# Attention and two mixtures on one core: transposes behind the first scores, the last root ahead of four scatters, and another last block

## The chip, the core and the metric

The kernel runs on one core of a Trainium2 chip. The core has a tensor engine (PE, with its weight loads shown apart as PEld), a vector engine (DVE), a scalar engine (ACT), GpSimd (POOL) and a queue engine (SP), each with its own instruction queue, worked through in order. Engines wait for one another by semaphores. The metric is the device time of one execution in microseconds (us).

## What is computed

```python
scores = np.where(mask, -1e9, scale * np.matmul(q, k.transpose(0, 1, 3, 2)))   # 4 x 12 heads, 448 x 448, 64 wide
attn = softmax(scores); x = np.matmul(attn, v)        # joined to x: 1792 rows of 768
# first mixture: 8 experts, w1 [8, 768, 1024], w2 [8, 1024, 768]
xn = x / (np.linalg.norm(x, axis=-1, keepdims=True) + 1e-06)
en = expert_emb / (np.linalg.norm(expert_emb, axis=-1, keepdims=True) + 1e-06)
logits = xn @ en.T / tau
# each row goes to the expert of its largest logit, gate_w is its probability
out[mask] = gate_w[mask, None] * (np.maximum(x[mask] @ w1[e], 0.0) @ w2[e])
# second mixture on that output: logits = x @ w_gate + modality_bias[modality_id], the same form
```

## The kernel before

All products are made of float32 numbers split into a high and a low part, so that one product is three matmuls (high by high, low by high, high by low). The order of the instructions is the order in which the program is written, on each engine.

**Attention.** A loop over `g` takes the 24 pairs of heads as a pipeline: in one round, `qk(g, c)` makes the scores of pair g in four chunks of 112 rows (L401 and, for the mask, L403 on PE), `rowmax` (L408, DVE) and `expo` (L413, ACT) follow them, `last_chunk` (transposes L435 on PE, `ph` L438 on ACT, `pl` L440 on DVE) and `values` (L468) work on earlier pairs, and `route_t` on a still earlier one. The scores stand in a pool of PSUM banks, and the transposes take two other banks in turn, one of which the embeddings' transposes (`enT_ps`) also use.

**Routing beside it.** What the first mixture needs for its choice of experts is written as generators, of which a round takes single steps with `tick()`. A `yield ALIGN` sets `hold`: the next step is only taken at `tick(True)`, which stands right behind the first two `qk` chunks of a round. `prep_en` normalizes the eight expert embeddings and transposes them on PE (L343); `route_root(b)` makes the reciprocal norms of batch b's rows from their sums of squares: for the last batch an add on DVE (L549), then `root2`, which starts with a power on POOL (L153, `rt_sr`) and goes on with small DVE instructions (L157, L159, L161, L163), and two more (L551, L553) that leave `r1nr`. The routing of a batch ends in scatters of its rows' places to a table in memory (L622 clears a column, L623 is the scatter on POOL).

**The mixtures.** Blocks of 128 rows that share an expert follow one another. A block's rows are gathered, transposed (L909), split into `xh` (ACT, L911) and `xl` (DVE, L912), multiplied with the first weights (L927, L928, L929, eight groups of 128 columns), and `down` multiplies with the second weights (`o`, L989), takes the gate in with two activations of 384 columns (L994, ACT) and scatters 128 rows of 768 to the output (L999, POOL). The first block of the first mixture opens while the routing of the last batch is being done; its `xl` stands on DVE behind `drain(route_root(B - 1))`, the root of the last batch.

**The end.** Sections run over up to 21 blocks, the last seven in nested tests of the number of blocks (L1306). With this data 17 blocks run. Behind the sections a flag `cl` tells whether the last block needs new second weights; the program tests it on all engines but PE (L1314) and splits them if so, and `down` for the last block follows on both ways.

Of the kernel before, what the change touches and what calls it, by code (L numbers as in the profile page):

```python
# [23 lines left out]
P = 128  # L24
# [31 lines left out]
def attention_two_moe_kernel(  # L56
# [225 lines left out]
    def drain(gen):  # L282
        for _ in gen:
            pass
# [42 lines left out]
    def prep_en():  # L327
        jk = xb_p.tile([CP, D], F32, tag="jk", name="ebj", bufs=2)[:E]
        ss = small.tile([E, 1], F32, tag="ess", name="ess")
        act.activation(jk, eb, AF.Square, accum_out=ss)  # L330
        yield
        nr = small.tile([E, 1], F32, tag="enr", name="enr")
        yield from root2(nr, ss, E, 1, "en")
        vec.tensor_scalar(out=nr, in0=nr, scalar1=0.5, scalar2=1e-6, op0=ALU.mult, op1=ALU.add)
        yield
        vec.reciprocal(nr, nr)
        yield
        vec.tensor_scalar_mul(jk, eb, nr)
        yield
        yield  # L340
        pt = ps_t.tile([P, KD, E], F32, tag="t", name="enT_ps")
        for c in range(KD):
            pe.transpose(pt[:, c], jk[:, c * P : (c + 1) * P], ident[:E, :E])  # L343
        yield
        for k in range(2):
            vec.tensor_copy(enT[:, :, k, :E], pt)
        vec.tensor_sub(enT[:, :, 0, E:], pt, enT[:, :, 0, :E].bitcast(F32))
        vec.tensor_copy(enT[:, :, 1, E:], zero8[:, None, :].to_broadcast([P, KD, E]))
# [179 lines left out]
    def route_ss(b, c, xb, part=0):  # L528

        cut = D - 2 * HD  # L530
        lo, hi = ((0, D), (0, cut), (cut, D))[part]
        if b not in sss:
            sss[b] = small.tile([CP, 2, NCH], F32, tag="r1ss", name=f"r1ss{b}")
        jk = xb_p.tile([CP, D], F32, tag="jk", name=f"r1jk{b}{c}{part}", bufs=2)
        acc = sss[b][:, part // 2, c : c + 1]
        if part == 2:
            vec.tensor_tensor_reduce(out=jk[:, lo:hi], in0=xb[:, c, lo:hi], in1=xb[:, c, lo:hi], scale=1.0, scalar=0.0,
                                     op0=ALU.mult, op1=ALU.add, accum_out=acc)
        else:
            act.activation(jk[:, lo:hi], xb[:, c, lo:hi], AF.Square, accum_out=acc)  # L540
# [140 lines left out]
    def split_w(which, his=None, los=None):  # L681
        drain(split_steps(which, his, los))
# [80 lines left out]
    for g in range(NPR + 3):  # L763
        t, v, r = g - 1, g - 2, g - 3
        if r == 0:
            drain(routing)
            routing = None
            vec.tensor_scalar_mul(tau_h, tau_t, 0.5)
            for b in range(B):
                vec.tensor_copy(mts[b][:, :, 3], mod_i[:, b * NCH : (b + 1) * NCH, 0])  # L770
        if 0 <= v < NPR and v % PB == 0:
            xbs[v // PB] = xb_p.tile([CP, NCH, D], F32, tag="xb", name=f"xb{v // PB}")
        late = [last_chunk(t, e) if 0 <= t < NPR else iter(()) for e in range(2)]
        if g < NPR:
            for c in range(2):
                qk(g, c)
        tick(True)
        if g < NPR:
            for c in range(2):
                both(rowmax, g, c)  # L780
            for c in range(2):
                both(expo, g, c, ticks=False)
        if g == NPR + 1:
            split_w(1, (), (2, 3))
        if g == NPR + 2:
            split_w(1, (), (4, 5))
        if 0 <= t < NPR:
            halves_lo(t)
        next(late[0], None)
        if NPR <= g:  # L790
            warm(ps_T, "T", WT)
        if 0 <= r < NPR:
            if r == NPR - 1:
                for c in range(NCH):
                    route_ss(B - 1, c, xbs[B - 1], 2)
            route_t(r, xbs[r // PB])
            if r == NPR - 2:
                for c in range(NCH):
                    route_ss(B - 1, c, xbs[B - 1], 1)
        next(late[0], None)  # L800
        if 0 <= v < NPR:
            if g > NPR - 1:
                warm(ps_T, "T", WV)
            values(v, 0)
        next(late[0], None)
        if PB <= r < NPR and r % PB < NCH:
            b = r // PB - 1
            c = -1
            for c in ((0,), (1,), (2,), (3,))[r % PB] if b < B - 2 else ((0,), (1,), (2, 3), ())[r % PB]:
                store_x(b, c)  # L810
                route_ss(b, c, xbs[b])
            if c == NCH - 1:
                drain(routing or ())
                routing = route1(b)
        if g < NPR:
            for c in range(2, NCH):
                qk(g, c)
                both(rowmax, g, c)
            for c in range(2, NCH):
                both(expo, g, c, ticks=False)  # L820
        next(late[1], None)
        if 0 <= v < NPR:
            values(v, 1)
        next(late[1], None)
        next(late[1], None)
        if 0 <= r < NPR:
            route_l(r)
        if 0 <= v < NPR:
            combine(v, xbs[v // PB])
        if g < NPR:  # L830
            halves_hi(g)
        if g + 4 < NPR:
            load_pair(g + 4)
        if g + 3 < NPR:
            load_v(g + 3)
        if g + 2 < NPR:
            split_pair(g + 2)
        if g + 1 < NPR:
            split_v(g + 1)
        if LEAD <= g <= NPR:  # L840
            for c in range(g - LEAD, KD if g == NPR else g - LEAD + 1):
                load_lead(m1, 1, c)
        if g == NPR - 1:
            st_q.close()
            ps_h = left("ps_h", 2, space=PSUM)
            ps_T = left("ps_T", 2, space=PSUM)
        if g == NPR:
            st_x.close()
            wb = left("wb", 1)
            w1h = [wb.tile([P, F], F32R, name=f"w1h{c}") for c in range(KD)]  # L850
            w1l = [wb.tile([P, F], F32R, name=f"w1l{c}") for c in range(KD)]
            w2r = [wb.tile([P, D], F32, name=f"w2r{f}") for f in range(KF)]
            m1.gather_early((0,), 2 * S)
            load_lead(m1, 2)
        if g == NPR:
            for k in range(2):
                pcopy(w1h[k], w1r[k])
            split_w(1, (2, 3, 4, 5), (0, 1))
# [24 lines left out]
    lgs2 = [wq.tile([P, 1, E], F32, name=f"lg{i}") for i in range(2)]  # L883
    mxs = [wq.tile([P, 1], F32, name=f"mx{i}") for i in range(2)]
    gt = wq.tile([P, MW], F32, name="gt")
    mes = [wq.tile([P, MW], F32, name=f"me{i}") for i in range(2)]
    KH = KF // 2
    hl, hh = ([wq.tile([P, KH, P], F32R, name=f"h{t}{i}") for i in range(2)] for t in "lh")
# [94 lines left out]
    def down(m, mg, then=None, between={}):  # L983
        ops = ps_a.tile([P, 2, 512], F32, tag="av", name="o")
        for f in range(KF):
            between.get(f, lambda: None)()
            for w, h, st in ((w2h, hh, 0), (w2l, hh, 1), (w2h, hl, 2)):
                for n in range(2):
                    pe.matmul(ops[:, n, :384], lhsT=h[f // KH][:, f % KH], rhs=w[f][:, n * 384 : (n + 1) * 384],  # L989
                              start=(f == 0 and st == 0), stop=(f == KF - 1 and st == 2))  # L990
        if then:
            then()
        for n in range(2):
            act.activation(yb[:, n * 384 : (n + 1) * 384], ops[:, n, :384], AF.Copy, scale=mg[:, 2:3])  # L994
        if m.routed:
            if then:
                pass_on()
            vec.tensor_copy(ym, mg)
        pool.indirect_dma_start(out=x1 if m.routed else out, out_offset=IND(ap=mg[:, 1:2].bitcast(I32), axis=0),  # L999
                                in_=yb, in_offset=None, bounds_check=NT - 1, oob_is_err=False)  # L1000

    def route_t2():
        for k in range(2):
# [229 lines left out]
    def run(m, is_full):  # L1233
# [72 lines left out]
        with ExitStack() as ifs:  # L1306
            for j in range(1, MAXB):
                if j == NBLK - 1:
                    total = nc.values_load(tab[0:1, 3, 0:1], min_val=NBLK, max_val=MAXB)
                    cl = nc.values_load(tab[0:1, 1, 0:1], engines=WE, min_val=0, max_val=1)  # L1310
                if j >= NBLK:
                    ifs.enter_context(tc.If(total > j))
                section(j)
        with tc.If(cl > 0):  # L1314
            split_w(2)
            if follow:
                load_lead(follow, 2)
        if follow:
            route_t2()
            follow.gather_early((0,), what="x")  # L1320
            split_w(1, range(3), ())
            drain(route_a())
            pass_on()
        if not follow:
            return down(m, gt)

        def middle():
            route_l2()
# [37 lines left out]
        yield  # L1366
        table(m1, None)

    drain(route_root(B - 1))
    m1.gather_early((1,), 3 * S)  # L1370
    open_phase(m1, m1.is_full(), last_route1, 2)
    is_full = run(m1, None)
# [41 lines left out]
```

## Time and profile before

| | |
|---|---|
| three runs | 974.64, 973.98, 970.02 us, median 973.98 |
| the profiled execution | 971.22 us, of it 969.5 from the first to the last instruction (the span) |
| mean granted clock of PE | 0.973 |
| busy in the span | PE 876.3, DVE 696.4, POOL 475.3, ACT 430.5 us |

Times in the profile are microseconds from the start of the span. A row of a timeline gives the start, the busy time, the engine with line and operation, output and inputs, and in brackets the idle time of the engine ahead of it with the instruction that ended it. A name with a q behind it (ACTq) is an engine's queue, where jumps, loads of registers and semaphores are.

### The profile page before, as it was taken

To read this page: it belongs to the slowest core of one execution; us is meant where nothing else is said; L and a number is where in the kernel's file an instruction comes from. 1 tells how busy PE (TensorE), PEld (TensorE's weight loads), DVE (VectorE), ACT (ScalarE), POOL (GpSimd) and SP (SyncE) were. 2 spreads that over 40 slices of the span, in tenths; PEclk is the share of its full clock that TensorE was granted. 3 is DMA by queue.
4 is the path that set the end of the run, shared out by engine and by line. 5 is a ranking of instruction groups with operands and counts; after the bars stand their busy time and mean duration, and the time that the engine had idled before them with its cause. 6 is when DMAs were issued, how large, how long until landed. Compare 5 with 4: busy or idle time off the path is not lost. (4 is left out here: it accounts for less than half of the span.)

```text
span 969.5 us, 20969 instructions
## 1 busy us (share of the span) xinstructions
PE 876.3 (90%) x7034; PEld 760.5 (78%) x7034; DVE 696.4 (72%) x1789; ACT 430.5 (44%) x777; POOL 475.3 (49%) x476
## 2 busy tenths in 40 slices
PE   5788898989868899999999999998989999899994
PEld 3677776767547788898989988886879998789894
DVE  6788888888764768689746965348767579996660
ACT  3565766857433565466525643234111234422111
POOL 8576655883135634464543564422545453463530
PEclk9999999999979899999999999999989999999997
DMA  6568796978915775468614662111172114411110
GB/s 186 121 134 164 159 188 130 197 179 167 262 47 183 283 291 177 172 222 307 223 45 165 221 205 83 46 33 38 53 266 82 50 52 165 152 51 38 63 40 31
DMA packets 112870, 137.45 MB, mean 142 GB/s; under 512 B 76800, under 2 KB 81200, under 8 KB 112704
## 3 DMA queue, kind: packets, MB, share of 16 engines
q1 hardware_dynamic: 99840, 108.75, 40.0%
q0 software_dynamic: 12864, 26.83, 8.7%
q8 instruction: 62, 1.02, 0.4%
q14 instruction: 104, 0.85, 0.3%
HBM read 101.48 MB, written 19.92 MB: 125 GB/s over the span
## 5 line engine op out<-in xcount | busy, mean ns | idle before, releaser
L728 POOL DMA_INDIRECT xg<-x,xi x128 | 134.1, 1047 | 99.0 <-DMA x<-yb,mg 50.1
L927 PE MATMUL h<-w1h,xh 128*128 128x512 f32 x408 | 165.9, 407 | 2.7 <-issue 1.9
L929 PE MATMUL h<-w1h,xl 128*128 128x512 f32 x408 | 162.2, 398 | 6.3 <-DVE xl L912 6.0
L928 PE MATMUL h<-w1l,xh 128*128 128x512 f32 x408 | 162.3, 398 | 3.0 <-DVEq L1226 2.6
L989 PE MATMUL o<-w2h,hh 128*128 128x384 f32 x544 | 145.4, 348 | 5.4 <-ACTq L1314 3.9
L989 PE MATMUL o<-w2l,hh 128*128 128x384 f32 x544 | 142.9, 344 | 4.9 <-issue 2.6
L989 PE MATMUL o<-w2h,hl 128*128 128x384 f32 x544 | 142.5, 343 | 2.3 <-issue 1.2
L969 DVE STREAM_TRANSPOSE hs<-h 32x256 f32<-32x256 f32 x240 | 107.0, 446 | 24.7 <-PE h L929 13.4
L413 ACT ACTIVATE ex<-sc,nm 112x112 f32<-112x112 f32 (+1 forms) x192 | 83.8, 492 | 76.5 <-DVE nm L408 75.3
L989 PEld LDWEIGHTS o<-w2l,hh 128*128 128x128 f32 x544 | 100.3, 192 | 6.9 <-issue 3.9
L989 PEld LDWEIGHTS o<-w2h,hh 128*128 128x128 f32 x544 | 98.9, 193 | 8.0 <-ACTq L1314 4.2
L989 PEld LDWEIGHTS o<-w2h,hl 128*128 128x128 f32 x544 | 100.7, 192 | 3.6 <-issue 1.8
L929 PEld LDWEIGHTS h<-w1h,xl 128*128 128x128 f32 x408 | 77.6, 190 | 25.3 <-DVE xl L912 6.8
L975 ACT ACTIVATE hh<-hs 128x512 fp32r<-128x512 f32 x30 | 18.5, 630 | 175.7 <-PE o L989 135.9
L928 PEld LDWEIGHTS h<-w1l,xh 128*128 128x128 f32 x408 | 77.8, 191 | 19.9 <-DVEq L1226 3.3
L927 PEld LDWEIGHTS h<-w1h,xh 128*128 128x128 f32 x408 | 77.9, 191 | 19.0 <-issue 3.7
L678 DVE TENSOR_TENSOR w1l<-w1r,w1h 128x1024 fp32r<-128x1024 f32 x66 | 76.6, 1220 | 11.3 <-issue 7.9
L408 DVE TENSOR_REDUCE nm<-sc 112x1 f32<-112x112 f32 (+1 forms) x192 | 75.6, 439 | 10.1 <-PE sc L403 9.5
L678 DVE TENSOR_TENSOR w2l<-w2r,w2h 128x768 fp32r<-128x768 f32 x82 | 72.5, 951 | 5.1 <-ACT w2h L676 3.8
L900 DVE STREAM_TRANSPOSE xr<-xg 128x768 f32<-128x768 f32 x32 | 52.1, 1628 | 30.9 <-DMA xg<-x,xi 18.7
L676 ACT CAST w1h<-w1r 128x1024 fp32r<-128x1024 f32 x64 | 62.5, 1046 | 11.1 <-DMA w1r<-in_w1a 3.7
L999 POOL DMA_INDIRECT out<-yb,mg x13 | 16.5, 1272 | 95.2 <-ACT yb L994 95.2
(296 smaller groups left out, 1936.3 us busy)
## 6 DMA issues: line engine op xcount, KB each, us to landing
w1r<-in_w1a SPq DMA_DIRECT2D x48, 512.0 KB
w2r<-in_w2a SPq DMA_DIRECT2D x64, 384.0 KB
r<-in_kqP SPq DMA_DIRECT2D x24, 448.0 KB
w1r<-in_w1b SPq DMA_DIRECT2D x18, 512.0 KB
w2r<-in_w2b SPq DMA_DIRECT2D x24, 384.0 KB
vr<-in_vh SPq DMA_DIRECT2D x24, 224.0 KB
x<-xb SPq DMA_DIRECT2D x16, 336.0 KB
xg<-x,xi POOLq DMA_INDIRECT x128
```

The source lines that it names most:

```text
L408: vec.tensor_reduce(out=nms[h][:, c : c + 1], in_=scs[h, c][:, : CP * (c + 1)], axis=AX.X, op=ALU.min)
L413: act.activation(dst, scs.pop((h, c))[:, :n], AF.Exp, bias=nms[h][:, c : c + 1], scale=-1.0)
L676: act.copy(hi[k], r[k])
L678: vec.tensor_sub(lo[k], r[k], hi[k].bitcast(F32))
L728: pool.indirect_dma_start(out=xgs[j % 3][:, q * (D // Q) : (q + 1) * (D // Q)], out_offset=None, in_=quarters, in_offset=IND(ap=xi[:, q : ...
L900: vec.transpose(xr.rearrange("p k (q r) -> p q k r", q=Q), xgs[j % 3].rearrange("p (q r k) -> p q k r", q=Q, k=KD))
L927: pe.matmul(hps, lhsT=xh[:, c], rhs=w1h[c][:, ns], start=(c == 0), stop=False)
L928: pe.matmul(hps, lhsT=xh[:, c], rhs=w1l[c][:, ns], start=False, stop=False)
L929: pe.matmul(hps, lhsT=xl[:, c], rhs=w1h[c][:, ns], start=False, stop=(c == KD - 1))
L969: vec.transpose(hr[cols, :, rows], hps[rows, q * 256 : (q + 1) * 256].rearrange("p (c k) -> p k c", c=QR))
L975: act.activation(hh[k], part, AF.Relu)
L989: pe.matmul(ops[:, n, :384], lhsT=h[f // KH][:, f % KH], rhs=w[f][:, n * 384 : (n + 1) * 384], start=(f == 0 and st == 0), stop=(f == KF - ...
```

## The change

Three edits. In `prep_en`, the second of two bare `yield`s becomes `yield ALIGN`. In the round where the last pair is routed, `route_root(B - 1)` is made and its first step taken ahead of `route_t`, and the old place drains the rest of it. At the end of the second mixture, `cl` is loaded on PE too, and the last block has its own `down_last`, written out in both ways of a test for `cl < 1`: all matmuls of the first 384 columns, then all of the second, each half with its own activation (the second into the tile `yT`) and its own scatter of 128 rows of 384 to the output seen as 3584 rows, by indices `two` = 2 x row + half.

```diff
@@ prep_en
-        yield
+        yield ALIGN
         pt = ps_t.tile([P, KD, E], F32, tag="t", name="enT_ps")
@@ the loop over g
             if r == NPR - 1:
                 for c in range(NCH):
                     route_ss(B - 1, c, xbs[B - 1], 2)
+                last_root = route_root(B - 1)
+                next(last_root)
             route_t(r, xbs[r // PB])
...
-    drain(route_root(B - 1))
+    drain(last_root)
@@ new
+    two = [wq.tile([P, 1], I32, name=f"two{i}") for i in range(2)]
+    def down_last(m, mg):
+        ops = ps_a.tile([P, 2, 512], F32, tag="av", name="o")
+        yhs = yb[:, :384], yT.rearrange("p k c -> p (k c)")[:, :384]
+        for n in range(2):
+            vec.tensor_scalar(out=two[n], in0=mg[:, 1:2].bitcast(I32), scalar1=2.0, scalar2=float(n), op0=ALU.mult,
+                              op1=ALU.add)
+        for n in range(2):
+            cols = slice(n * 384, (n + 1) * 384)
+            for f in range(KF):
+                for w, h, st in ((w2h, hh, 0), (w2l, hh, 1), (w2h, hl, 2)):
+                    pe.matmul(ops[:, n, :384], lhsT=h[f // KH][:, f % KH], rhs=w[f][:, cols],
+                              start=(f == 0 and st == 0), stop=(f == KF - 1 and st == 2))
+            act.activation(yhs[n], ops[:, n, :384], AF.Copy, scale=mg[:, 2:3])
+            i = pool.indirect_dma_start(out=out.rearrange("n (k d) -> (n k) d", k=2), out_offset=IND(ap=two[n], axis=0),
+                                        in_=yhs[n], in_offset=None, bounds_check=2 * NT - 1, oob_is_err=False)
+            apart(i.ins, "out")
@@ run
-                    cl = nc.values_load(tab[0:1, 1, 0:1], engines=WE, min_val=0, max_val=1)
+                    cl = nc.values_load(tab[0:1, 1, 0:1], engines=WE if follow else WE + [ENG.PE], min_val=0, max_val=1)
...
+        if not follow:
+            with tc.If(cl < 1) as same:
+                down_last(m, gt)
+            with same.Else():
+                split_w(2)
+                down_last(m, gt)
+            return
         with tc.If(cl > 0):
             split_w(2)
-            if follow:
-                load_lead(follow, 2)
+            load_lead(follow, 2)
...
-        if not follow:
-            return down(m, gt)
```

On PE, this is the program at the start of pair 2, before: the transposes of the embeddings (L343) stand between a transpose of pair 1 (L435) and the first scores of pair 2.

```order
L435 MATMUL t<-ident,ex_211 112x112 x4
L343 MATMUL enT_ps<-ident,ebj 128x8 x6
L401 MATMUL sc_0_505<-hi_392 112x112
L401 MATMUL sc_0_506<-hi_392 112x112
L401 MATMUL sc_0_505<-lo_393,hi_392 112x112
```

And with the change, the rows at the other end of those scores: L343 has moved behind all 20 rows of the chunks 0 and 1, ahead of the next transpose L435.

```order
L403 LDWEIGHTS identb
L403 MATMUL sc_1_508<-mask,identb 112x112
L403 LDWEIGHTS identb
L403 MATMUL sc_1_509<-mask,identb 112x112
L343 MATMUL enT_ps<-ident,ebj 128x8 x6
L435 MATMUL t<-ident,ex_212 112x112 x4
```

On POOL, this is the queue ahead of the first mixture, before: two splits of first weights (L143), four clears and scatters of the batch ahead of the last, and the power of the last batch's root (L153) behind them.

```order
L143 TENSOR_SCALAR w1h_5530<-w1r_314 128x1024
L143 TENSOR_SCALAR w1h_5531<-w1r_315 128x1024
L622 MEMSET pad 128x1
L623 DMA meta_63<-mt_115,r1sir_5771 14336x8
L622 MEMSET pad 128x1
L623 DMA meta_63<-mt_115,r1sir_5771 14336x8
L622 MEMSET pad 128x1
L623 DMA meta_63<-mt_115,r1sir_5771 14336x8
L622 MEMSET pad 128x1
L623 DMA meta_63<-mt_115,r1sir_5771 14336x8
L153 TENSOR_TENSOR rt_sr_5891<-r1ss_5623,half 112x4
```

And with the change: the power stands ahead of all eight (on DVE, L549 moves with it, from behind L272 to ahead of L507).

```order
L143 TENSOR_SCALAR w1h_5530<-w1r_314 128x1024
L143 TENSOR_SCALAR w1h_5531<-w1r_315 128x1024
L153 TENSOR_TENSOR rt_sr_5794<-r1ss_5623,half 112x4
L622 MEMSET pad 128x1
L623 DMA meta_63<-mt_115,r1sir_5771 14336x8
```

On ACT, the end of the program with the change: behind the test (L1336, the place of L1314 before) come the two halves of the way without new weights, a jump, and the other way. Before, the eight casts (L676) stood in the test alone, and the two activations (L994) behind it.

```order
L1336 COMPARE_AND_BRANCH
L1018 ACTIVATE yb<-o,gt 128x384
L1018 ACTIVATE yT<-o,gt 128x384
L1336 UNCONDITIONAL_BRANCH
L676 CAST w2h_5887<-w2r_5542 128x768
```

## Rows read from the trace of the kernel before

**Rows 1.** Page, busy us, share of the span, instructions

```profile
PE 876.3 (90%) x7034; PEld 760.5 (78%) x7034; DVE 696.4 (72%) x1789; ACT 430.5 (44%) x777; POOL 475.3 (49%) x476
```

**Rows 2.** Waits of PE in the attention, 0 to 265 (total, times, longest)

```profile
PE t L435 <- DVE xb L487: 10.5, 15, 0.8
```

**Rows 3.** Timeline of PE at the start of pair 2

```profile
29.92 0.81 PE L343 MATMUL enT_ps<-ident,ebj 8*128 8x8 f32 x6 [6.43 <-DVE pl L440]
...
31.76 0.53 PE L401 MATMUL sc<-hi 64*112 64x224 f32 x2
...
32.59 0.44 PE L403 MATMUL sc<-mask,identb 112*112 112x112 bf16 x2
```

**Rows 4.** Timeline of PE in the first block of the first mixture

```profile
272.37 0.77 PE L927 MATMUL h<-w1h,xh 128*128 128x512 f32 x1
272.94 0.63 PE L928 MATMUL h<-w1l,xh 128*128 128x512 f32 x1
279.62 0.80 PE L929 MATMUL h<-w1h,xl 128*128 128x512 f32 x1 [6.05 <-DVE xl L912]
```

**Rows 5.** Timeline of DVE ahead of that block

```profile
268.56 0.62 DVE L507 TENSOR_TENSOR xTl<-t,xTh 128x448 fp32r<-128x448 f32 x1
...
271.62 0.14 DVE L549 TENSOR_TENSOR r1ss<-r1ss 112x4 f32<-112x4 f32 x1
277.18 0.17 DVE L157 TENSOR_SCALAR rt_rr<-rt_sr 112x4 f32<-112x4 f32 x1 [5.41 <-POOL rt_sr L153]
...
277.79 0.16 DVE L163 TENSOR_TENSOR r1nrr<-rt_rr,rt_sr 112x4 f32<-112x4 f32 x1
...
279.00 1.02 DVE L912 TENSOR_TENSOR xl<-xt,xh 128x384 fp32r<-128x384 f32 x2 [0.57 <-DVE r1nrr L553]
```

**Rows 6.** Timeline of PE, start of the last block's second product

```profile
949.53 1.01 PE L989 MATMUL o<-w2h,hh 128*128 128x384 f32 x2 [3.91 <-ACTq L1314]
```

**Rows 7.** Timeline of DVE around pair 2

```profile
23.36 1.70 DVE L163 TENSOR_TENSOR enr<-rt_ren,rt_sen 8x1 f32<-8x1 f32 x1
...
29.24 0.62 DVE L440 SCALAR_TENSOR_TENSOR pl<-t,ph 112x448 f16<-112x448 f32 x1 [1.13 <-ACT ph L438]
...
31.13 0.18 DVE L348 CAST enT<-zero 128x48 fp32r<-128x48 f32 x1
...
32.97 0.69 DVE L408 TENSOR_REDUCE nm<-sc 112x1 f32<-112x224 f32 x2 [0.74 <-PE sc L403]
```

**Rows 8.** Timeline of POOL around pair 2

```profile
22.98 2.07 POOL L146 TENSOR_TENSOR lo<-r,hi 128x896 fp32r<-128x896 f32 x1
```

**Rows 9.** Timeline of ACT around pair 2

```profile
28.14 0.63 ACT L413 ACTIVATE ex<-sc,nm 112x448 f32<-112x448 f32 x1 [0.93 <-DVE nm L408]
```

**Rows 10.** Timeline of POOL ahead of the first mixture

```profile
271.31 1.03 POOL L623 DMA_INDIRECT meta<-mt,r1sir  x1 [20.54 <-DVE ld_rowm L268]
...
276.11 1.04 POOL L153 TENSOR_TENSOR rt_sr<-r1ss,half 112x4 f32<-112x4 f32 x1
```

**Rows 11.** Windows: length, busy of each engine (instructions), PE clock, DMA share, GB/s

```profile
269.39:283.04 13.65, 6.97 (x26) 4.51 (x25) 6.23 (x40) 3.07 (x6) 5.29 (x9) 0.50 0.05 15
949.53:955.48 5.95, 5.95 (x19) 5.79 (x19) 0.00 (x0) 0.00 (x0) 0.00 (x0) 0.50 0.05 19
955.48:960.90 5.42, 5.42 (x31) 5.09 (x30) 0.00 (x0) 0.00 (x0) 0.00 (x0) 1.00 0.00 0
963.80:965.00 1.20, 0.00 (x0) 0.00 (x0) 0.00 (x0) 0.00 (x0) 0.00 (x0) 1.00 0.64 259
```

**Rows 12.** Queue instructions of L1309 (ns min/median/max, first and last start)

```profile
L1309 PEldq TENSOR_LOAD <-t_tabm x1: 308/308/308, 892.3 to 892.3; - x1
```

**Rows 13.** Queue instructions of L1306 from 940 to 952

```profile
L1306 PEldq COMPARE_BRANCH  x2: 186/1820/3453, 942.3 to 946.0; - x2
...
L1306 ACTq EVENT_SEMAPHORE  x2: 17/17/17, 949.0 to 949.1; - x2
L1306 DVEq EVENT_SEMAPHORE  x2: 21/21/21, 949.5 to 949.6; - x2
```

**Rows 14.** Timeline of ACT at the end

```profile
960.99 1.05 ACT L994 ACTIVATE yb<-o,gt 128x384 f32<-128x384 f32 x2 [14.05 <-PE o L989]
```

**Rows 15.** Queue instructions of L1410, end of the program, 960 to 970

```profile
L1410 POOLq DRAIN  x3: 46/113/6547, 962.1 to 969.2; - x3
```

**Rows 16.** Waits of PE from 283 to 345, the longest

```profile
PE h L927 <- issue: 1.9, 2, 1.1
PE pr L1044 <- DVE oh L199: 1.2, 1, 1.2
```

## The prediction

> **What bounds the kernel now.** The page comes first [rows 1]: PE, the tensor engine, is busy for 876 of 969.5 us, so the time can only fall where PE stands idle or runs slowly, and each part of the change is priced at the idle stretch of PE that it touches. The waits of PE in the attention (0 to 265 us) show one of 0.7 us in each of fifteen pairs, on DVE's L487 [rows 2]; they return with the loop, so what PE gains in one pair isn't waited away in the next. The other views are timelines at three places. *Pair 2*: PE stands idle for 6.43 us ahead of the embeddings' transposes, L343 [rows 3]. *Opening of the first mixture*: PE waits 6.05 us ahead of the first L929 [rows 4], for `xl` on DVE (L912), which ends a chain that waited 5.41 us for POOL's power `rt_sr` (L153) [rows 5]. *End*: 3.91 us of idle ahead of the last block's matmuls [rows 6], and a serial tail behind them.
>
> **Part (a), ALIGN in `prep_en`.** Nothing is added or removed. Six transposes (0.81 us) go from ahead of the first two QK chunks of pair 2 to behind them, and three casts on DVE go behind one row maximum. The transposes need the PSUM bank that `pl` (L440) frees at 29.24+0.62 = 29.86 [rows 7]; the QK chunks, which stand behind them, don't. They run from the transposes' end, 29.92+0.81 = 30.73, to 32.59+0.44 = 33.03 [rows 3]. When could they run? Their operands are split by POOL at 22.98+2.07 = 25.05 [rows 8]. Chunk 0 needs two score banks that ACT's exponentials free early, chunk 1 the one that the exponential of 28.14+0.63 = 28.77 frees [rows 9]. So chunk 0 goes into the idle stretch whole, and chunk 1 starts at 28.8 and takes 33.03-31.76 = 1.27 [rows 3]: 30.07. The transposes, by then free of their wait, end at 30.85, where QK ended at 33.03 before: 2.2 us less, of which **I take 2.0** for a start 0.2 later. The casts on DVE ended 31.13+0.18-30.73 = 0.58 behind the transposes [rows 7], so now at 31.4, and hold chunk 1's maximum until about 31.65; before it started at 32.97 [rows 7]. DVE and ACT thus gain 1.3 where PE gains 2.0, and if they pace pair 2, 1.3 is what stays. Bounds: 0 (pairs 3 and 4 wait for loads or splits instead) and 2.2.
>
> **Part (b), the last root ahead of the scatters.** On POOL the power goes past four memsets and the four scatters from 271.31 to just ahead of 276.11, where it took 1.04; POOL had been idle for 20.54 us before them [rows 10]. Its input, the sums of squares, is complete when DVE reaches L507 at 268.56; the add L549, 0.14 us, now comes ahead of that [rows 5]. So the power runs from 268.75 to 269.8, in idle time. DVE's six instructions from L157 on keep their place behind that of L549, where DVE is free at 271.62; they start there and not at 277.18, 5.5 us earlier, take 1.25 us to 278.43 as before (L912 at 279.00 follows the last by 0.57), and `xl` starts at about 273.45 [rows 5]. Its other input, `xh`, is a cast of PE's transposes and is done by 273: PE's first matmul on it ran at 272.37 and the next at 272.94 [rows 4]. PE's L929 goes to about 274.15 from 279.62 [rows 4]: **5.4 us**. Costs: 0.14 for the add ahead of L507, since PE waits for L507's `xTl`; and the power now runs beside DVE's L507. How such a pair fares: L163 on 8 numbers took 1.70 us at 23.36 [rows 7] while POOL's subtraction `lo` ran from 22.98 to 25.05 [rows 8]; the same line took 0.16 at 277.79 with POOL at rest [rows 5]. DVE is held for as long as POOL works, here at most 1.04 us. I take 0.25 of it, since L507 starts with the power or ahead of it and has one input in PSUM: **5.0 us**. The scatters end 1.1 us later, at 277.1; PE waits for none of them by [rows 4, 16], and the next scatters hang on the chain that has moved forward, as all of the last batch's route does.
>
> The Trainium skill ("SBUF — State Buffer", SBUF: two separate sides) states the same as an exclusive lock between a GpSimd operation and a DVE operation with two SBUF inputs, held for the whole instruction; the rows agree (1.70 against 0.16), and by it in full this part would give 5.4-0.14-1.04 = 4.2 in place of 5.0.
>
> The clock adds a bound. PE was granted 0.50 (1.2 GHz) from 269.39 to 283.04 [rows 11], until 3.42 us behind its restart at 279.62. With less idle ahead of it, the return can come earlier behind the restart, or later. The last block prices it: 19 matmuls in 5.95 us at 0.50 and 31 in 5.42 at 1.00 [rows 11], 0.313 against 0.175 each, so a us at the low level does 0.56 us of work, and 3.42 us can give 1.5 back. I take nothing. Bounds of (b): 3.6 (block and add in full, and 0.6 for a later return) and 6.9.
>
> **Part (c), the last block.** One scalar load on PE is added at section 13, 0.31 us by the one beside it [rows 12], under matmuls that are queued there; uncovered it would cost those 0.31. *Start:* PE was ready after its own jump (3.453 us, begun at 942.3 under matmuls) and a branch of 0.19 at 946.0 [rows 13], so at 946.2, and waited for ACT behind L1314 until 949.53 [rows 6]. ACT's events of the sections jumped over come at 949.0 and 949.1, and DVE's, which only the second matmul wants, at 949.5 [rows 13]. Now the test behind L1314 falls through and those events are enough: PE starts near 949.1, **0.4 earlier**. Two new index operations on DVE lie under 11 us of matmuls. *Order:* the 48 matmuls are the same, half after half; the low clock of their first 5.95 us stays, and where it falls can move up to 19 x (0.313-0.175) = 2.6 either way; I take nothing. *Tail:* ACT evicted two halves in 1.05 behind the last matmul [rows 14]; the first now lies under the second half's matmuls, **0.5 less**. The scatter behind it moves half the bytes. Before, packets ran for about 1.2 us at 259 GB/s [rows 11], so this is worth 0.6 if the drain on POOL, from 962.1 for 6.547 us [rows 15], ends with the landing, and 0 if it counts from its start. I take **0.25**. Sum 1.15; bounds 0.5 and 1.5 without the clock.
>
> **Sum.** -2.0 -5.0 -1.15 = -8.15. From the profiled execution's time, 971.22, that gives 963.1; from the median of the three runs, 973.98, it gives 965.8. The profiled execution lies inside those runs (970.02 to 974.64), so I take the middle of the two: **964.4**, from a start of 972.6.
>
> **Rivals.**
> *1. (b) is half given back:* PE gets `xl` early, but some us on it waits for what doesn't hang on the root: splits of the second weights on ACT and DVE, gathers on POOL. For it: those engines do a long list of work there, and their loads were issued on time for the old start. Against: PE's waits from 283 to 345 are 1.2 us and less [rows 16], so no second wait lies close behind the first. -5.65: 966.9.
> *2. (a) carries nothing:* the next pairs are paced by splits on POOL, which fill it there [rows 8]. Against: all that PE waits for later in the attention are the 0.7 us of [rows 2]. -6.15: 966.4.
> *3. The change doesn't do what it says in (b):* the power also reads sums that ACT accumulates, and stands in POOL's queue behind splits of the first weights; if one of them is late, DVE waits on as before. Against: POOL had done with those splits 20.54 us before its scatters [rows 10]. -3.15: 969.4, within 0.5%.
> *4. The other side, PE's clock.* The thin work of 270 to 274 now lies directly ahead of the dense work, and 1.2 GHz may last longer than 3.42 us behind the restart. Each such us loses 0.44. After 18.5 us of longer low clock, to about 296, the 8.15 are gone; past 30 us, to about 307, the kernel is over 0.5% slower, 979 or more. Against it: after the longer idle of before, the high level was back 3.42 us behind the restart [rows 4, 11].
> *5. Better:* the clock returns at once in (b), -1.5 more: 962.9.
>
> The new jumps are a risk inside the range: a jump of 3.453 us on PE, ready at 946.2, would put its start to 949.65 and cost 0.55 [rows 13]. The Trainium skill ("Runtime: NRT & Kernel Launch", Instruction fetch mechanics) states that a taken branch to a target outside the fetched window stalls for the fetch; that row agrees, 3.453 beside a branch of 0.19, and one such stall on PE's new branch would make the sum 7.6 in place of 8.15.
>
> **Chances.** Forecast (963 to 966) 0.50; rival 1 0.18; rival 2 0.12; rival 3 0.09; rival 4 0.03; rival 5 0.08. About 0.5%, 4.9 us, is what a measurement of this kernel can tell from no change: faster is below 969.1. Forecast and rivals 1, 2 and 5 make 0.88, of which 0.04 (the slow edges of 1 and 2) falls to no change: faster 0.84, same 0.13, slower 0.03. The range, 960.5 to 969.0, leaves out rivals 3 and 4 and the far edge of 5.
>
> **What would show it.** (a): L343 stands behind QK chunk 1, no idle of 6.4 us ahead of it, and pair 2 ends some 2 us earlier, as does the attention. (b): POOL's L153 near 269 for about 1.05 us; no wait of 5.4 at L157; the 6.05 ahead of L929 under 1. (c): PE's idle ahead of the last block near 3.5 us, and one eviction behind the last matmul. I'm wrong where such a wait is only renamed: idle of PE of like size within 40 us behind it, or a low clock that lasts much beyond 279.

## The result: 965.6 us, 0.991 of before, and where it came from

The changed kernel took 965.61 us (median of 20 runs, 959.33 to 971.42), the one before, beside it, 973.93 (20 runs, 967.82 to 980.4). The ratio is 0.9913, 95% interval 0.9892 to 0.9933: faster by 8.3 us, more than 0.5%. Forecast were 964.4 us in a range of 960.5 to 969.0. A second measurement on another chip gave 0.9939 (0.9915 to 0.9963), 5.9 us: so the gain is 6 to 8 us, and that the first measurement lies within 0.2 us of the forecast's 8.15 is in part luck.

The profiled execution of the changed kernel has a span of 966.8 us at a mean granted clock of 0.967, against 969.5 at 0.973. These 2.7 us are not the gain, since the two executions differ in their clock where the change has no part. From 40 to 262 us the changed kernel's has 20.5 us at the low level (0.50 granted) and the other 6.8; from 600 to 940 us it has 10.2 against 13.7. At the 0.44 us that the prediction reckons lost in a us at the low level, that is an estimated 4.5 us against the changed kernel. So the places are compared one by one, each from a mark near it. The page:

```profile
PE 881.5 (91%) x7034; PEld 761.0 (79%) x7034; DVE 698.4 (72%) x1791; ACT 430.2 (44%) x777; POOL 472.4 (49%) x477
```

**Pair 2.** Timeline of PE, to be read beside [rows 3]:

```profile
24.58 0.69 PE L401 MATMUL sc<-hi 64*112 64x112 f32 x2 [1.44 <-ACT ex L413]
...
27.27 0.52 PE L401 MATMUL sc<-hi 64*112 64x224 f32 x1 [1.18 <-ACT ex L413]
...
28.46 0.80 PE L343 MATMUL enT_ps<-ident,ebj 8*128 8x8 f32 x6
29.19 0.99 PE L435 MATMUL t<-ident,ex 112*112 112x112 f32 x4
```

The idle stretch of 6.43 us is gone from ahead of L343. In its place stand two waits for ACT's exponentials, 1.44 and 1.18 us, which free the score banks: chunk 0 needed them too, not only chunk 1. DVE in the same place, beside [rows 7]:

```profile
28.22 0.27 DVE L408 TENSOR_REDUCE nm<-sc 112x1 f32<-112x112 f32 x1
29.30 0.32 DVE L346 CAST enT<-enT_ps 128x48 fp32r<-128x48 f32 x2 [0.81 <-PE enT_ps L343]
29.54 0.21 DVE L347 TENSOR_TENSOR enT<-enT_ps,enT 128x48 fp32r<-128x48 f32 x1
29.66 0.18 DVE L348 CAST enT<-zero 128x48 fp32r<-128x48 f32 x1
29.75 0.86 DVE L408 TENSOR_REDUCE nm<-sc 112x1 f32<-112x112 f32 x3
```

The casts stand between the first row maximum and the other three, as the order said, and hold them: DVE waits 0.81 us for PE's transposes, while the scores of chunk 0's second head are ready. The mark for this place is ACT's second copy `ph` (L438), which comes ahead of pair 2, and from it to PE's next L435 it takes 4.16 us before and 2.08 now:

```profile
28.67 0.54 ACT L438 ACTIVATE ph<-t 112x448 f16<-112x448 f32 x1
32.83 0.95 PE L435 MATMUL t<-ident,ex 112*112 112x112 f32 x4
```

```profile
27.11 0.54 ACT L438 ACTIVATE ph<-t 112x448 f16<-112x448 f32 x1
```

**Opening of the first mixture.** POOL, DVE and PE, beside [rows 10], [rows 5] and [rows 4]:

```profile
271.55 1.04 POOL L153 TENSOR_TENSOR rt_sr<-r1ss,half 112x4 f32<-112x4 f32 x1 [22.11 <-DVE r1ss L549]
...
274.17 1.05 POOL L623 DMA_INDIRECT meta<-mt,r1sir  x1 [1.52 <-DVE ld_rowm L268]
```

```profile
271.24 0.16 DVE L549 TENSOR_TENSOR r1ss<-r1ss 112x4 f32<-112x4 f32 x1
271.32 0.62 DVE L507 TENSOR_TENSOR xTl<-t,xTh 128x448 fp32r<-128x448 f32 x1
271.86 0.18 DVE L176 TENSOR_TENSOR fr_shr<-r1lgr,am_mxr 112x32 f32<-112x32 f32 x1
...
274.48 0.15 DVE L157 TENSOR_SCALAR rt_rr<-rt_sr 112x4 f32<-112x4 f32 x1
...
276.27 1.02 DVE L915 TENSOR_TENSOR xl<-xt,xh 128x384 fp32r<-128x384 f32 x2 [0.57 <-ACT xh L914]
```

```profile
275.79 0.63 PE L931 MATMUL h<-w1l,xh 128*128 128x512 f32 x1
276.88 0.80 PE L932 MATMUL h<-w1h,xl 128*128 128x512 f32 x1 [0.47 <-issue]
```

The power runs in POOL's idle time, L157 waits for nothing, and 6.05 us of idle are 0.47. The attention of this execution ended 2.85 us later than that of before (ACT's copy `lgs`, L519, at 272.58 against 269.73), so the mark is that copy: from it to `xl` 9.27 us before (269.73 to 279.00) and 3.69 now, 5.58 less; the add ahead takes 0.1 to 0.2 of it. L507 and L176 ran beside the power and were not held. The copy, before and now:

```profile
269.73 0.52 ACT L519 COPY lgs<-lg 16x448 f32<-16x448 f32 x1 [2.94 <-PE lg L516]
```

```profile
272.58 0.52 ACT L519 COPY lgs<-lg 16x448 f32<-16x448 f32 x1 [3.24 <-PE lg L516]
```

No wait of like size follows: in the 40 us behind the restart PE's longest wait is 0.83 us, where it was 1.10.

**The end.** PE, ACT and POOL's queue, beside [rows 6], [rows 14] and [rows 15]:

```profile
947.22 0.58 PE L1016 MATMUL o<-w2h,hh 128*128 128x384 f32 x1 [2.93 <-ACTq L1327]
...
953.07 0.34 PE L1016 MATMUL o<-w2h,hl 128*128 128x384 f32 x1
954.21 0.44 PE L1016 MATMUL o<-w2h,hh 128*128 128x384 f32 x1 [0.80 <-ACT yb L1018]
...
958.36 0.34 PE L1016 MATMUL o<-w2h,hl 128*128 128x384 f32 x1
```

```profile
953.57 0.58 ACT L1018 ACTIVATE yb<-o,gt 128x384 f32<-128x384 f32 x1 [7.96 <-PE o L1016]
958.74 0.58 ACT L1018 ACTIVATE yT<-o,gt 128x384 f32<-128x384 f32 x1 [4.58 <-PE o L1016]
```

```profile
L1435 POOLq DRAIN  x3: 46/113/6452, 959.5 to 966.5; - x3
```

Three things: PE's idle is 2.93 in place of 3.91; a new wait of 0.80 stands between the two halves, for ACT's eviction of the first; and from the last matmul's end (958.70) to the end of the span it takes 8.1 us, where it took 8.6. The drain on POOL lasts 6.45 us from 959.5, with half the bytes behind it, as it lasted 6.55 with all of them.

### The profile page after: what moved, and what is told of

The parts are those of the page before. It is cut to its first block, busy times and chain, and to the rows that moved or that the text cites. A ratio compares the mean times of both kernels' runs of the same rounds, so it can differ in the third digit from the quotient of the medians.

```text
span 966.8 us, 20984 instructions
## 1 busy us (share of the span) xinstructions
PE 881.5 (91%) x7034; PEld 761.0 (79%) x7034; DVE 698.4 (72%) x1791; ACT 430.2 (44%) x777; POOL 472.4 (49%) x477
## 5 line engine op out<-in xcount | busy, mean ns | idle before, releaser
L992 PE MATMUL o<-w2l,hh 128*128 128x384 f32 x528 | 136.8, 340 | 4.6 <-DVE w2l L678 2.4
L992 PE MATMUL o<-w2h,hh 128*128 128x384 f32 x528 | 139.4, 345 | 1.8 <-issue 1.6
L992 PE MATMUL o<-w2h,hl 128*128 128x384 f32 x528 | 137.3, 341 | 3.3 <-issue 2.8
L992 PEld LDWEIGHTS o<-w2l,hh 128*128 128x128 f32 x528 | 95.8, 189 | 7.1 <-issue 3.7
L992 PEld LDWEIGHTS o<-w2h,hl 128*128 128x128 f32 x528 | 96.4, 190 | 3.6 <-issue 2.5
L992 PEld LDWEIGHTS o<-w2h,hh 128*128 128x128 f32 x528 | 95.1, 190 | 4.8 <-issue 2.9
L678 DVE TENSOR_TENSOR w1l<-w1r,w1h 128x1024 fp32r<-128x1024 f32 x66 | 76.5, 1220 | 13.7 <-ACT w1h L676 11.8
L676 ACT CAST w1h<-w1r 128x1024 fp32r<-128x1024 f32 x64 | 62.3, 1046 | 12.8 <-DMA w1r<-in_w1a 6.2
```

The costliest lines, as they stand in the source:

```text
L676: act.copy(hi[k], r[k])
L678: vec.tensor_sub(lo[k], r[k], hi[k].bitcast(F32))
```

## The experiments

All ratios are to the kernel before on the same chip; that kernel's own median differs between chips (964 to 974), so times are not compared between chips. A ratio here is not the quotient of the two medians.

**Each part alone.** The three kernels are the change with two of its three edits undone. The first:

```diff
         vec.tensor_scalar_mul(jk, eb, nr)
         yield
-        yield
+        yield ALIGN
```

> Only the ALIGN in prep_en. Theory 1 (each part gives its own): no idle of 6.4 us ahead of L343, in its place two waits on ACT's exponentials of 1.4 and 1.2 us, pair 2 and all behind it 2 to 4 us earlier, and the time 2 to 3 us less than before (ratio 0.997 to 0.998). Rival (the root alone carries the change): the attention gets shorter in the trace, but what follows waits for weights or gathers, and the time is within 1 us of before.

Measured: 961.51 against 964.29 us, ratio 0.9982 (0.9948 to 1.0016). The interval takes in both the theory and the rival, so the time alone settles nothing. In the trace PE's L435 of pair 2 comes 2.05 us earlier than in the next kernel, profiled on the same chip with the old order (31.17 against 33.22), but by 97 us only 0.9 are left, and at the end of the attention 0.5 (by ACT's `ph`). Two things stand in the trace that can have taken it. DVE, with POOL beside it:

```profile
31.64 1.00 DVE L348 CAST enT<-zero 128x48 fp32r<-128x48 f32 x1
32.56 0.86 DVE L408 TENSOR_REDUCE nm<-sc 112x1 f32<-112x112 f32 x3
```

```profile
31.56 1.03 POOL L146 TENSOR_TENSOR r<-vr 112x512 f32<-112x512 f32 x1
```

The cast of zeros, 0.18 us in the changed kernel's trace above, here ends with POOL's instruction, 0.8 us late, and with it the three row maxima. And PE's clock: the first product of the fourth score chunk of this execution, and of one of the same attention (the changed kernel once more, below):

```profile
36.29 0.71 PE L401 MATMUL sc<-hi 64*112 64x448 f32 x2
```

```profile
36.48 0.46 PE L401 MATMUL sc<-hi 64*112 64x448 f32 x2
```

The same two matmuls at the low and at the high level. In the first 32 to 40 us PE runs at the low one (in the changed kernel's first trace with 3.4 us at the high one between), and the rise comes at another time in each execution: here at 39.8 us by the spacing of the matmuls, in the next kernel near 37, which at 0.44 a us is an estimated 1.2. How much of the loss each of the two took is not shown.

The second:

```diff
+                last_root = route_root(B - 1)
+                next(last_root)
             route_t(r, xbs[r // PB])
...
-    drain(route_root(B - 1))
+    drain(last_root)
```

> Only the early root. Theory 1: the wait of 5.4 us at L157 is gone, L929 follows its predecessor within 0.6 us in place of 6.05, and the time is 5 us less (ratio 0.995). Rival (the root alone carries the change): 7 to 8 us less (ratio 0.992). A second rival, that half of it is given back by waits in the next blocks: 2 to 3 us less (0.997).

Measured: 958.28 against 964.29 us, ratio 0.9939 (0.9913 to 0.9966), 5.9 us less. The interval, 3.3 to 8.4 us, holds the theory's 5 and leaves out the second rival's 2 to 3; the first rival's 7 to 8 lie in it, and only the trace speaks against them: from `lgs` to `xl` 3.70 us, 5.57 less than before.

The third has `down_last`, the flag on PE and the test in both ways, with the first two edits undone:

```diff
-        if not follow:
-            return down(m, gt)
+        if not follow:
+            with tc.If(cl < 1) as same:
+                down_last(m, gt)
+            with same.Else():
+                split_w(2)
+                down_last(m, gt)
+            return
```

> Only the new last block. Theory 1: PE starts the last block's second product 0.4 us earlier behind the jump, ACT evicts one half behind the last matmul (0.5 less), but the second half's first matmul waits 0.8 us for ACT's eviction of the first, as in the changed kernel, and the drain on POOL takes 6.5 us from its own start whatever the bytes: 0 to 0.6 us less, ratio 0.999 to 1.000. Rival (the prediction's sum): 1.15 us less, ratio 0.9988, no idle between the halves.

Measured: 961.54 against 964.29 us, ratio 0.9977 (0.9952 to 1.0002): lower than either said, with both in the interval, so the time can't part them. The trace has the gap of 0.80 between the halves and 8.1 us behind the last matmul, as the theory says; PE's idle is 2.95, about 1 us less than before where 0.4 were expected.

The three parts alone add to 1.0% (0.18, 0.61 and 0.23), beside the 0.87% and 0.61% that the whole gave: within these intervals the parts add.

**The last root, two scatters later.** `next(last_root)` taken inside the loop of the scatters:

```diff
+            if b == 2 and c == 2:
+                next(last_root)
             pool.memset(pad, 0.0)
```

> The kernel before with the last root's add and power put behind two of the four scatters instead of ahead of all. Theory (the wait at L157 is the queue ahead of the power on POOL, 1.25 us a scatter): the wait of DVE falls from 5.41 by two scatters, 2.5 us, to 2.9, and PE's idle ahead of the block's third matmul from 6.05 to about 3.5. Rival (any early power would do, since something else sets the chain): no wait of DVE, and PE's idle near 0.5.

DVE and PE in its trace:

```profile
276.99 0.17 DVE L157 TENSOR_SCALAR rt_rr<-rt_sr 112x4 f32<-112x4 f32 x1 [2.92 <-POOL rt_sr L153]
```

```profile
279.51 0.80 PE L932 MATMUL h<-w1h,xl 128*128 128x512 f32 x1 [3.65 <-DVE xl L915]
```

2.92 against 2.9 expected, and PE's idle 3.65 against 3.5; from `lgs` to `xl` 6.87 us, between 9.27 and 3.69. The wait is the queue ahead of the power on POOL, scatter by scatter. (Its single run, 968.03, is no measurement of 2.5 us.)

**Taking the last block apart.** First the halves with the old test, an edit of the kernel before:

```diff
         if not follow:
-            return down(m, gt)
+            return down_last(m, gt)
```

> The kernel before with the two halves and scatters of the last block, but with the old test ahead of them (L1314 skips the splits by a jump, no load of the flag on PE). Theory (the test written out in both ways makes PE start earlier, the halves only change the tail): idle ahead of the last block's second product 3.9 us as before and not the 2.95 of the new test, 0.8 us between the halves, 8.1 us from the last matmul's end to the end of the span in place of 8.6. Rival (the start has nothing to do with the test): 2.95 here too.

```profile
946.11 0.44 PE L1014 MATMUL o<-w2h,hh 128*128 128x384 f32 x1 [3.80 <-ACTq L1333]
947.05 0.69 PE L1014 MATMUL o<-w2l,hh 128*128 128x384 f32 x1 [0.50 <-DVEq L1333]
...
953.40 0.44 PE L1014 MATMUL o<-w2h,hh 128*128 128x384 f32 x1 [0.72 <-ACT yb L1016]
```

The long idle is back, and with it a second wait, for DVE; the gap is 0.72, and 8.12 us follow the last matmul, so the theory holds and the rival doesn't. (One run, 967.74 beside a median of 969.75.) Then the test alone, the third kernel of the parts with `down` as it was before:

```diff
             with tc.If(cl < 1) as same:
-                down_last(m, gt)
+                down(m, gt)
             with same.Else():
                 split_w(2)
-                down_last(m, gt)
+                down(m, gt)
```

> The kernel before with the new test alone at the end: flag loaded on PE too, the last block written out in both ways, but with the old order of matmuls, two activations behind the last matmul and one scatter of 128x768. Theory (the start and the tail are two separate gains): idle ahead of the last block's second product 2.7 to 3.1 us as in the changed kernel and not 3.8 to 4.6; no gap in the matmuls; 8.6 us from the last matmul's end to the end of the span, as before. Rival (the earlier start comes with the halves' order): 3.8 or more here too.

```profile
944.08 0.62 PE L990 MATMUL o<-w2h,hh 128*128 128x384 f32 x2 [2.67 <-ACTq L1307]
944.95 1.01 PE L990 MATMUL o<-w2l,hh 128*128 128x384 f32 x2 [0.25 <-DVEq L1307]
```

2.67 us, no gap, 8.65 behind the last matmul, as the theory said. (One run, 965.02, beside one of the kernel before, 964.32: no measurement.) Third, the changed kernel with the second half in a PSUM tile of its own:

```diff
-        ops = ps_a.tile([P, 2, 512], F32, tag="av", name="o")
+        ops = ps_a.tile([P, 2, 512], F32, tag="av", name="o")[:, 0], ps_T.tile([P, 512], F32, tag="T", name="o1")
```

> The changed kernel with the second half of the last block accumulated in a PSUM tile of its own (one that the transposes used before). Theory 1 (the 0.8 us ahead of the second half is a wait on the shared PSUM tile): that idle is gone, the two halves follow each other without a gap, and the time is 0.8 us below the changed kernel: 0.9905 to 0.991 of before. Rival (the matmul waits for something else of the first half, such as weights or the index operations): the gap stays 0.8 us.

```profile
939.23 0.34 PE L1016 MATMUL o<-w2l,hh 128*128 128x384 f32 x1
939.40 0.34 PE L1016 MATMUL o<-w2h,hl 128*128 128x384 f32 x1
939.58 0.34 PE L1016 MATMUL o<-w2h,hh 128*128 128x384 f32 x1
```

The last matmul of the first half (939.40) and the first of the second (939.58) follow each other as all others do: the 0.8 us were a wait on the shared tile. Measured 953.72 against 964.29, ratio 0.9886 (0.9849 to 0.9922, 6 runs): below the 0.9905 to 0.991 expected, and 0.8 us can't be read from such an interval.

What the block takes from the end of the product ahead of it to the end of the span, in all traces, with the time at the low clock priced at the 0.44 of its length that the prediction worked out:

| last block | idle | low clock | tail | sum less 0.44 of low |
|---|---|---|---|---|
| old (4 traces) | 3.89 to 4.55 | 3.4 to 5.9 | 8.58 | 21.3 to 21.9, mean 21.5 |
| halves, old test | 3.80 | 3.4 | 8.12 | 22.2 |
| new test alone | 2.67 | 3.4 | 8.65 | 20.4 |
| the change (3 traces) | 2.73 to 2.95 | 3.4 to 6.1 | 8.1 | 20.95 to 21.1 |
| the change, own tile (2) | 2.71, 3.13 | 3.4 | 8.1 | 20.1, 20.4 |

By these sums, which spread by 0.3 us within a row, the test gives 1.1 us, the halves as written lose 0.6, and the change as a whole gives 0.5. With a tile of its own the wait between the halves is gone, though little stands above the test alone (20.1 and 20.4 beside 20.4, of one trace).

**The changed kernel again, and one with three mends** (own tile; casts behind all four maxima; the cast of zeros at the start of the program):

> The changed kernel once more, beside the next one on the same chip. By what was measured of it: ratio 0.989 to 0.993. In its trace the rise of PE's clock in the first pairs is looked at: pair 2 is 2 us earlier at L435 in any case, and what is left of it at 100 us is 0.5 to 4 us by where the rise falls (theory); the rival, that the transposes' place alone sets what is left, says 2 us within 0.5.

```diff
     def prep_en():
+        vec.tensor_copy(enT[:, :, 1, E:], zero8[:, None, :].to_broadcast([P, KD, E]))
...
-        yield
+        for _ in range(4):
+            yield
         for k in range(2):
             vec.tensor_copy(enT[:, :, k, :E], pt)
         vec.tensor_sub(enT[:, :, 0, E:], pt, enT[:, :, 0, :E].bitcast(F32))
-        vec.tensor_copy(enT[:, :, 1, E:], zero8[:, None, :].to_broadcast([P, KD, E]))
```

> The changed kernel with three more edits: the last block's second half in a PSUM tile of its own; the embeddings' casts on DVE behind all four row maxima of pair 2; the clear of a part of enT (a cast of zeros, SBUF to SBUF) at the start of the program. Theory: the 0.8 us between the halves is gone; the maxima of pair 2 no longer wait for the casts, nor the cast for POOL, so pair 2's exponentials come 1 us earlier than in the changed kernel: 1 to 2 us below it, ratio to before 0.988 to 0.990. Rival: the attention is paced by PE, its gain there is nil, and only the 0.8 us at the end are left, 0.9905.

Measured on one chip, against 969.75: the changed kernel 963.31 (0.9939, 0.9915 to 0.9963), the mended one 962.28 (0.9910, 0.9881 to 0.9938). Both ratios lie above what was expected (0.989 to 0.993 and 0.988 to 0.990), and the second nearer to its rival's 0.9905. Its maxima and casts on DVE:

```profile
31.24 1.04 DVE L409 TENSOR_REDUCE nm<-sc 112x1 f32<-112x112 f32 x4
32.32 0.32 DVE L348 CAST enT<-enT_ps 128x48 fp32r<-128x48 f32 x2
```

All four maxima run without a wait, and the second `ph` to the third takes 3.11 us, 0.9 to 1.7 less than with the other four traces of the new order; but to the twelfth it takes 47.14, which is in their range, so this gain is not seen later. The medians differ by 1 us and the intervals overlap: that the mended kernel beats the changed one is not shown.

What (a) is worth, from all traces: from ACT's second L438 (`ph`, ahead of pair 2) to its twelfth, the kernels with the old order took 48.4 to 49.6 us (before, the early root alone, the new block alone, two of the block's parts and the root behind two scatters; mean 48.9), those with the new order 46.5 to 48.3 (47.23, 48.32, 47.43, 46.54; mean 47.4). To the 26th, with no low clock on record until then, the means are 116.4 and 114.9. So it gives 1.5 us by the means, with single traces 0.9 to either side of that. From the second `ph` to L435 of pair 2 the old order took 4.14 to 4.16 us in every trace and the new 2.08 to 2.09: the 2.06 at L435 are always there, and half a us of them is lost behind it on average. That the clock's rise takes it is not shown: the traces of the old order alone spread by 1.2 us, and the rival's 2 us within 0.5 takes in the mean.

## Why the prediction was right, and where its terms were off

**The whole:** -8.15 forecast, -8.3 measured, chances on the right side. The terms by the traces: (a) 1.5 for 2.0, (b) 5.4 for 5.0, (c) 0.5 for 1.15, together 7.4 (7.9 with the estimate for the clock below). The interval of the ratio, 0.0067 to 0.0108 of 973.9, is 6.5 to 10.5 us, so the traces' 7.4 and the forecast both lie in it. The sum was as good as it was because its terms err in both directions, which is luck, and the second measurement's interval, 0.9915 to 0.9963, holds the forecast's 0.9916 only just.

**(a), mis-sized.** L435 of pair 2 came 2.05 earlier in the pair of traces from one chip, as said. What was left behind it was nearer to the 1.3 that was given for DVE and ACT: the second `ph` to the third took 5.4 us in every trace of the old order and 3.99 to 4.81 in the new. The step that failed is the choice of PE's 2.0 over their 1.3 where both had been worked out. (That chunk 0 waits too, 1.4 to 3.2 us, cost nothing at L435, which follows the second `ph` by 2.08 or 2.09 us however long that wait was.) Not foreseen: the cast of zeros beside POOL, up to 0.8 us, and where the clock's rise falls. The prediction says nothing of the clock in the first pairs; the rows that it moved there are at the low level.

**(b), right.** Place, size and order of events were as written: power in idle time, L157 right behind L272, PE's wait to 0.47. The 0.25 for a block by POOL didn't come: L507 and L176 took 0.62 and 0.18 beside the power, as without it. The Trainium skill ("SBUF — State Buffer", SBUF: two separate sides) would have held L176, which has two inputs in SBUF, as long as the power ran; here the measurement decides: it was not held, in any of the five traces with the early root, and the part gave more than the 4.2 of that rule. The cast L348 of the first experiment, SBUF to SBUF, was held until POOL's instruction ended (1.00 us against 0.18), as the Trainium skill says in the same place of such copies. The kind of the DVE operation does not part the two cases, for L163, with two inputs in SBUF too, was held 1.70 us [rows 7]. POOL's instruction differs: 112x4 numbers beside L176, 112x512 and 128x896 beside the ones that were held; which of its properties decides stays open. The low clock lasted 4.88 us behind the restart, not 3.42:

```profile
271.52:281.76 10.24, 8.67 (x29) 5.77 (x30) 8.03 (x43) 3.07 (x6) 5.42 (x10) 0.50 0.11 35
276.88:281.76 4.88, 4.88 (x16) 3.56 (x17) 4.81 (x27) 0.31 (x1) 1.99 (x4) 0.50 0.02 2
```

At 0.44 a us that is 0.6 against the change in this execution, but the 3.42 were the exception: the four other traces with the root in its old place have 5.8 to 6.2 us of low clock behind the restart, the five with it ahead of all scatters 2.5 to 5.3. By the means, 5.5 and 4.4, the clock gave the change an estimated 0.5 us, which with the 5.4 makes the 5.9 of the early root alone. The 3.42 that the prediction took came from one trace, and the shortest; rivals 4 and 5 both stayed away in size. Rival 1 (half given back, 2.5 us left) is refuted by the early root alone, at least 3.3 us less, and by PE's waits of 0.83 us and less in the 40 us behind the restart; rival 3 by the missing wait. (The 979 of rival 4 starts from 973.98; from the sum's 972.6 it is 977.7.)

**(c), right in kind, wrong in three of four terms.** *Start:* 1.0 in this pair of traces (2.93 for 3.91), 1.1 by the table, and not 0.4. Of that, 0.45 is the event behind L1314 as foreseen; the rest is that ACT's jump itself took 2.8 us (944.4 to 947.2) where it took 3.3 (945.7 to 949.0) [rows 13]. That is no accident of one trace: ACT's events come 3.3 to 4.1 us behind the end of the product ahead in the five traces with the old test and 2.6 to 3.2 in the six with the new. Why is open. No stall came on PE's new branch (0.33 at most). *Order:* "the 48 matmuls are the same, half after half" missed that both halves lie in one tile: the second half's first matmul, which writes the tile that ACT is reading, waited 0.8 us. This wait, which the sum put at nothing, is the step that failed in (c), and it is about what parts the change from the kernels with a tile of their own in the table (21.0 and 20.1 to 20.4). *Tail:* 0.5 as said. *Bytes:* nothing for 0.25; the drain lasts 6.5 us from its start. Start, order and tail add to 0.8, and the table's 0.5 agrees within its spread.

## What to carry to other kernels

A small instruction on a queue of another engine can cost the length of that queue: ask of each wait on a quick helper what stands ahead of the helper, and move its first step, not the chain behind it; here one power on 112x4 numbers, moved ahead of four scatters, gave most of the gain. Splitting a product so that its eviction hides needs a tile for each half; in one tile the second half waited 0.8 us here for the eviction of the first. And before two profiles are compared, compare their granted clocks, stretch by stretch: with 0.006 less of mean clock, the profiled pair shows 2.7 us of a gain of 6 to 8.

## What was not expected of the hardware

The clock's first rise: in the first pairs, matmuls ran at low-level speed in every trace (0.71 us for the two of 64x448 at 20.9 to 22.4 us, 0.46 later on). Yet the profile's windows print 1.00 there, since the clock's records begin later, at 35 to 40 us in ten of the eleven traces. The first profile of the changed kernel has a record of it, and so 3.4 us of its lost clock are ones that the others lost too and don't show:

```profile
25.76:32.59 6.83, 5.65 (x66) 5.03 (x67) 4.88 (x13) 4.19 (x9) 6.58 (x6) 0.50 0.46 87
```

Between executions the time at the low clock from 40 to 262 us varied from 6.8 to 23.9 us without any edit there that explains it; whether the new order in pair 2 has a part in it (mean 17.9 in four traces with it, 13.7 in six without) stays open. The end of the program took 8.1 to 8.65 us behind the last matmul in all kernels, of which 6.4 to 6.6 were POOL's drain, whether 128x768 or 128x384 numbers were still to be written.
